# Decode attention and MLP on one core: load targets moved to multiples of 512 bytes, wo read four rows to a partition, the last V in quarters, h1's zeros written early

## The chip, the cores and the metric

The kernel runs on one core of a Trainium2 chip, the other cores idle. The metric is the device time of one execution in microseconds (us), the median of three runs. A profiled execution of the same kernel gives the trace; its span runs from the first instruction to the last.

## The reference

One decoding step of a pre-LayerNorm transformer block: four sequences, one new token each, 32 heads of 128, 4096 cached positions.

```python
x = A_x                                               # (4, 1, 640), all bf16
h = x + attention(_layernorm(x), k_cache, v_cache, wq, wo)
h2 = h + mlp(_layernorm(h), w1, b1, w2)               # the result

def attention(x, k_cache, v_cache, wq, wo):           # caches (4, 32, 4096, 128), wq (640, 4096)
    q = (x @ wq).reshape(B, 1, 32, 128).transpose(0, 2, 1, 3)
    p = softmax(einsum("bhqd,bhkd->bhqk", q, k_cache) * 128 ** -0.5)
    o = einsum("bhqk,bhkd->bhqd", p, v_cache)
    return o.transpose(0, 2, 1, 3).reshape(B, 1, 4096) @ wo    # wo (4096, 640)

def mlp(x, w1, b1, w2):                               # w1 (640, 1728), w2 (1728, 640)
    h = x @ w1 + b1
    return (h * tanh(log1p(exp(-abs(h))) + max(h, 0))) @ w2
```

The two caches are 134 MB each, so nearly all of the work is reading them once.

## The kernel before

**Tiles.** A group `g` (of `NG` = 32) is one sequence and four heads. `load_k(g)` and `load_v(g)` (lines 85 to 100) each bring 4 MB into a tile of 128 partitions by 32 KB: partition `32*q + p` holds 128 successive positions of head `q`. There are two K and two V buffers. For the last group alone, K and V come in `NP` = 2 parts, so that work can start on the first.

**One group.** `mul_and_sum` multiplies K by the broadcast query on VectorE (line 334) and sums over the head's 128 elements by matmuls with the identity (line 341); `finish_sum` and `softmax` make the weights `e2`; `pv_moving` (line 242) multiplies V as the moving operand. For groups 30 and 31 `pv` (line 268) is used: 128 matmuls, one for each position of a partition, V as weights.

**Projection.** `normalise(hq)` writes `otn[:, hq]`, the attention output of four heads with the element `d` on the partitions. `project(hq)` (line 315) adds 20 matmuls to `yT`, with `wo_sb[:, h, :]` as weights, in which partition `p` holds row `128*h + p` of wo. `PROJ_AT` says after which group each `project` runs. wo is loaded in four DMAs after groups 8 to 11 (line 431), eight heads each. A DMA moves one contiguous run at a time; here a run is one row of wo, 1,280 bytes.

**The queue of loads.** All loads but x are issued by SyncE's queue (SP), in program order: wq, then K and V by turns, wo and b1 between them, and at the end (lines 460 to 464) w1, `w2s_sb` (160 KB), `w2r_sb` (the last 64 rows of w2, 80 KB) and w2 in three parts of 640 KB. K of group `g+2` can be issued only when group `g` has been used up, since it overwrites it. The 16 DMA engines each carry 8 partitions of a 128-partition load and work through their own list in order.

**Completion semaphores.** In the built program the loads of SP's queue take eight completion semaphores by turns. A load that takes a semaphore waits, on SP, until the load that had it eight places earlier has landed on all engines. In the tail before, V31's parts have numbers 7 and 0, w1 1, `w2s_sb` 2, `w2r_sb` 3; the parts of w2 have 4, 5 and 6, which the two halves of K31 and V30 had.

**The tail** (lines 467 to 597): softmax of group 31, `pv(30)`, `pv(31)`, `normalise(7)`, `project(7)`, the residual `hT`, its mean (line 488), `h2T` (line 495), 70 matmuls with w1 into `h1_ps` (line 511), the activation, 70 matmuls with w2 into `y2T` (line 573: first `w2s_sb`, then `w2r_sb`, then the three parts of w2), and the store. The last chunk of `h1_ps` has only 64 rows of weights; a memset (line 506) writes zeros in its other 64 rows, and the first matmul of line 511 comes after that memset.

**Where the loads land.** In the built program of before, a partition holds the small constants first, then wq, then the working tiles, then K and V. K starts at byte 93,088 of a partition, which is 160 bytes past a multiple of 256 and 32 past one of 64; the other K and V buffers and `w12` (w1 and w2, in a K buffer) stand the same way. wq and wo start at 48,416 (32 past a multiple of 256, and of 64). `x_bf`, 5 KB, starts at 16,512: a multiple of 128, and not of 256.

Of the kernel before, what the change touches and what calls it, by code (L numbers as in the profile page):

```python
# [8 lines left out]
FP32 = mybir.dt.float32  # L9
BF16 = mybir.dt.bfloat16  # L10
# [6 lines left out]
def kernel(  # L17
# [23 lines left out]
    nc = tc.nc  # L41

    B, Sq, D = A_x.shape
    _, H, Sk, Dh = A_k_cache.shape
    F = B_w1.shape[1]
    N = B * Sq
    DC = D // 128
    G = 4
    PH = 128 // G
    R = Sk // PH  # L50
    NP = 2
    RP = R // NP
    W = 512 // RP
    HQ = H // G
    NG = HQ * N
# [3 lines left out]
    WOC = 8  # L59
# [9 lines left out]
    C2 = F // 128  # L69
    FREM = F - C2 * 128  # L70
    FC = C2 + 1

    ctx.enter_context(tc.manual_schedule())

    consts = ctx.enter_context(tc.tile_pool(name="consts", bufs=1))
    wbig = ctx.enter_context(tc.tile_pool(name="wbig", bufs=1))
    work = ctx.enter_context(tc.tile_pool(name="work", bufs=2))
    kpool = ctx.enter_context(tc.tile_pool(name="kpool", bufs=KBUFS))
    vpool = ctx.enter_context(tc.tile_pool(name="vpool", bufs=VBUFS))

    x_rows = A_x.rearrange("b s d -> (b s) d")
    out_rows = out.rearrange("b s (c p) -> (b s c) p", p=128)


    def load_kv(pool, tag, cache, g):
        hq, b = divmod(g, N)
        t = pool.tile([128, R, Dh], BF16, tag=tag, name=f"{tag}{g}")
        view = cache[b, G * hq : G * (hq + 1)].rearrange("h (p r) d -> (h p) r d", p=PH)

        np_ = NP if g == NG - 1 else 1  # L90
        for i in range(np_):
            r0, r1 = i * R // np_, (i + 1) * R // np_
            nc.sync.dma_start(out=t[:, r0:r1, :], in_=view[:, r0:r1, :])
        return t

    def load_k(g):
        return load_kv(kpool, "kt", A_k_cache, g)

    def load_v(g):
        return load_kv(vpool, "vt", A_v_cache, g)  # L100

    x_bf = consts.tile([N, D], BF16)
    nc.scalar.dma_start(out=x_bf[:, :], in_=x_rows[:, :])
# [9 lines left out]
    ident = consts.tile([128, 128], BF16)  # L113
# [20 lines left out]
    otn = consts.tile([128, HQ, N, G], BF16)  # L134

    for q in range(G):
        nc.vector.tensor_copy(
            out=sel[:, :, q, q * PH : (q + 1) * PH],
            in_=ident[0:N, 0:N].unsqueeze(2).to_broadcast([N, N, PH]),
# [27 lines left out]
    ps = ps_cm.__enter__()  # L167
# [51 lines left out]
    PROJ_AT = {B1_AT + 1 + hq: hq for hq in range(4)}  # L219
# [70 lines left out]
    def normalise(hq):  # L290
        nc.vector.tensor_tensor(
            out=otn[:, hq, :, :],
            in0=ot.pop(hq)[:, :, :],
            in1=rls.pop(hq)[:, :, :],
            op=ALU.mult,
        )
# [3 lines left out]
    def f_chunk(rows, c):  # L300

        if c < CK * CI:
            k, i = divmod(c, CI)
            block = rows[:, k * 128 * CI : (k + 1) * 128 * CI]
            return block.rearrange("p (f i) -> p i f", i=CI)[:, i, :], 128
        return rows[:, c * 128 : min(F, (c + 1) * 128)], min(F - c * 128, 128)

    yT = ps.tile([128, DC, N], FP32, tag="yT")
    wo_sb = []

    def project(hq):

        for h in range(hq * G, (hq + 1) * G):
            for c in range(DC):
                nc.tensor.matmul(
                    yT[:, c, :],
                    lhsT=wo_sb[0][:, h, c * 128 : (c + 1) * 128],
                    rhs=otn[:, hq, :, h % G],
                    start=(h == 0 and c == 0),
                    stop=(h == H - 1 and c == DC - 1),  # L320
                )
# [3 lines left out]
    def mul_and_sum(g, part):  # L325

        hq, b = divmod(g, N)
        r0 = part * RP
        kt = kts[g][:, r0 : r0 + RP, :]
        s_ps = ps.tile([128, RP, W], FP32, tag="s", bufs=2, name=f"s{g}_{part}")  # L330
        s_of[g, part] = s_ps
        for k in range(NQ):
            d0 = k * DQ
            nc.vector.tensor_tensor(  # L334
                out=kt[:, :, d0 : d0 + DQ],
                in0=kt[:, :, d0 : d0 + DQ],
                in1=qbs[:, hq, b, d0 : d0 + DQ].unsqueeze(1).to_broadcast([128, RP, DQ]),
                op=ALU.mult,
            )
            for d in range(d0, d0 + DQ, W):  # L340
                nc.tensor.matmul(  # L341
                    s_ps[:, :, :],
                    lhsT=ident[:, :],
                    rhs=kt[:, :, d : d + W],
                    start=(d == 0),
                    stop=(d == Dh - W),
                )
            yield

    def finish_sum(g, part):  # L350
        if part == 0:
            s_sbs[g] = work.tile([128, R], FP32, tag="s_sb", name=f"s_sb{g}")
        nc.vector.tensor_reduce(  # L353
            out=s_sbs[g][:, part * RP : (part + 1) * RP],
            in_=s_of.pop((g, part))[:, :, :],
            axis=AX.X,
            op=ALU.add,
        )
# [35 lines left out]
    for g in range(NG):  # L394
        hq, b = divmod(g, N)
        for part in range(NP):
            now = mul_and_sum(g, part)
            before = None
            next(now)
            if part > 0:  # L400
                finish_sum(g, part - 1)
                if 2 <= g < NG - NSTAT + 2:
                    add_blocks(g - 2)
                    if b == 1:
                        row_sums(hq - 1)
                        normalise(hq - 1)
            elif g >= 1:
                finish_sum(g - 1, NP - 1)
                before = softmax(g - 1)
                next(before)  # L410
            next(now)
            if before is not None:
                next(before)
        kts.pop(g)
        if g + 2 < NG:
            kts[g + 2] = load_k(g + 2)
        if 1 <= g < NG - NSTAT + 1:
            pv_moving(g - 1)
        if g in PROJ_AT:
            project(PROJ_AT[g])  # L420
        if g + 1 < NG:
            vts[g + 1] = load_v(g + 1)
        for n in Q_AT.get(g, ()):
            q_chunk(n)
            q_broadcast(n)
        if g in WO_AT:

            if not wo_sb:
                wo_sb.append(wbig.tile([128, H, D], BF16, tag="w", name="wo_sb"))
            h0 = WO_AT[g] * WOC  # L430
            nc.sync.dma_start(
                out=wo_sb[0][:, h0 : h0 + WOC, :],
                in_=A_wo.rearrange("(h p) n -> p h n", p=128)[:, h0 : h0 + WOC, :],
            )
            if WO_AT[g] == 0:
                nc.sync.dma_start(out=b1_row[:, :], in_=B_b1.rearrange("(o f) -> o f", o=1))
        if g == B1_AT:
            b_ps = ps.tile([128, FC], FP32, tag="small", name="b_ps")
            for c in range(FC):
                cols, fw = f_chunk(b1_row[:, :], c)  # L440
                nc.tensor.matmul(
                    b_ps[0:fw, c : c + 1],
                    lhsT=cols,
                    rhs=ident[0:1, 0:1],
                    start=True,
                    stop=True,
                )
            nc.vector.tensor_copy(out=b1T[:, 0:C2], in_=b_ps[:, 0:C2])
            nc.vector.tensor_copy(out=b1T[0:FREM, C2:FC], in_=b_ps[0:FREM, C2:FC])
# [7 lines left out]
    w2r_sb = mlp.tile([FREM, D], BF16)  # L457
# [1 line left out]
    w2_view = B_w2[0:FM, :].rearrange("(k p i) n -> p k i n", k=CK, i=CI)  # L459
    nc.sync.dma_start(out=w1_sb, in_=B_w1.rearrange("(c p) n -> p c n", p=128))  # L460
    nc.sync.dma_start(out=w2s_sb[:, :], in_=B_w2[FM : C2 * 128, :])
    nc.sync.dma_start(out=w2r_sb[:, :], in_=B_w2[C2 * 128 : F, :])
    for k in range(CK):
        nc.sync.dma_start(out=w2_sb[:, k], in_=w2_view[:, k])


    finish_sum(NG - 1, NP - 1)
# [26 lines left out]
    for dst in (h2T, hc):  # L494
        nc.vector.tensor_tensor(
            out=dst[:, :, :],
# [5 lines left out]
    nc.vector.tensor_tensor(out=sq[:, :, :], in0=hc[:, :, :], in1=hc[:, :, :], op=ALU.mult)  # L502


    h1_ps = ps.tile([128, FC, N], FP32, tag="qq", name="h1_ps")
    nc.vector.memset(h1_ps[FREM:128, FC - 1, :], 0.0)
    rstd = mlp.tile([128, N], FP32)
    for c in range(FC):
        fw = f_chunk(w1_sb[:, 0, :], c)[1]
        for dc in range(DC):  # L510
            nc.tensor.matmul(  # L511
                h1_ps[0:fw, c, :],
                lhsT=f_chunk(w1_sb[:, dc, :], c)[0],
                rhs=h2T[:, dc, :],
                start=(dc == 0),
                stop=(dc == DC - 1),
            )
        if c == 4:
# [3 lines left out]
                out=std[:, :], in_=v_ps[:, :], func=ACT.Sqrt, bias=eps_t[:, :], scale=1.0  # L522
# [5 lines left out]
        out=h1n[:, :, :],  # L528
# [6 lines left out]
        out=h1s[:, :, :],  # L535
# [9 lines left out]
        out=tb[:, :, :],  # L545
# [8 lines left out]
        out=ta[:, :, :], in0=tb[:, :, :], scalar1=-0.5, scalar2=-1.0, op0=ALU.mult, op1=ALU.add  # L554
# [4 lines left out]
        out=act_t[:, :, :],  # L559
# [10 lines left out]
    for i, (w2, c) in enumerate(w2_of):  # L570
        rows = 128 if c < C2 else FREM
        for dc in range(DC):
            nc.tensor.matmul(  # L573
                y2T[:, dc, :],
                lhsT=w2[:, dc * 128 : (dc + 1) * 128],
                rhs=act_t[0:rows, c, :],
                start=(i == 0 and dc == 0),
                stop=(i == FC - 1 and dc == DC - 1),
# [3 lines left out]
        out=oT[:, :, :].rearrange("p n c -> p c n"),  # L582
# [7 lines left out]
        lhsT=oT[:, :, :].rearrange("p n c -> p (n c)"),  # L590
        rhs=ident[:, :],
        start=True,
        stop=True,
# [35 lines left out]
```

## Time and profile before

| what | us |
|---|---|
| median of three runs (674.6 to 674.92) | 674.84 |
| the profiled execution, whole | 674.36 |
| its span | 672.6 |
| PE busy / DVE busy in the span | 566.7 / 351.6 |

The span is 1.8 us shorter than the execution that it belongs to: start and end lie outside it.

The trace also holds each DMA packet (here one contiguous run) with its time on its engine:

| run | what | packets | shortest, ns | median, ns | mean, ns |
|---|---|---|---|---|---|
| 40,960 B | wq | 128 | 1,514 | 1,514 | 1,605 |
| 32,768 B | K, V | 7,936 | 1,213 | 1,215 | 1,218.5 |
| 16,384 B | halves of K31, V31 | 512 | 611 | 613 | 616 |
| 5,120 B | w2 in three parts | 384 | 196 | 201 | 215 |
| 3,456 B | w1 (and b1) | 641 | 135 | 140 | 145 |
| 1,280 B | wo | 4,096 | 55 | 59 | 59.6 |
| 1,280 B | `x_bf` | 4 | 53 | 53 | 90 |

All 397 K and V packets that began before 44 us took 1,213 ns. In that stretch the next packet of an engine starts 3 to 4 ns before the one ahead of it ends.

And when each load of the tail had landed on its first and on its last engine, by the completion semaphores:

| load | first engine, us | last engine, us |
|---|---|---|
| V30 | 641.2 | 646.4 |
| V31, first half | 646.1 | 651.3 |
| V31, second half | 651.0 | 656.26 |
| w1 | 656.4 | 662.09 |
| `w2s_sb` | 656.9 | 662.69 |
| `w2r_sb` | 657.3 | 663.18 |
| w2, parts 1, 2, 3 | 659.0, 660.6, 662.4 | 664.50, 666.07, 667.63 |

The engines are 5 to 6 us apart there. For w1, six of the 16 landed between 661.4 and 662.09, three at 659.8 to 660.0 and seven between 656.4 and 658.8.

### The profile page before, as it was taken

The page shows a single profiled execution, that of the slowest core. Times are in us where ns is not written, and L with a number is a line of the kernel's source. Part 1 is how long each engine was busy: PE and PEld are TensorE (multiplying, and loading weights), DVE is VectorE, ACT ScalarE, POOL GpSimd, SP SyncE. Part 2 cuts the span into 40 slices and gives each one's busy share as a digit, 9 for nine tenths or more (in the row PEclk, how much of TensorE's full clock was granted, in tenths as well). Part 3 has the DMA queues.
Part 4 walks back from the last instruction along what each step waited for, and adds up shares of the span by engine and source line. Part 5 has one row for each costly group of instructions (what it writes and reads, how often), then busy time and mean ns, then how long its engine had stood idle before and what let it go on. Part 6 is the DMA issues. An engine that isn't in the chain of part 4 may idle for free.

```text
span 672.6 us, 7163 instructions
## 1 busy us (share of the span) xinstructions
PE 566.7 (84%) x3121; PEld 256.1 (38%) x3121; DVE 351.6 (52%) x304; ACT 112.2 (17%) x343; POOL 2.4 (0%) x13
## 2 busy tenths in 40 slices
PE   0589999899998896688999899879988799888985
PEld 0234444344443332233443344333433344333454
DVE  2475445455654356236654545665544566554642
ACT  0022122122210111011110111111111111101231
POOL 1000000000000000000000000000000000000000
PEclk9999999799998987878998899898999799898995
DMA  9999999999999999999999999999999999999995
GB/s 373 437 436 437 430 428 428 426 437 434 432 431 421 422 416 412 441 419 425 430 434 427 433 430 430 431 435 432 431 428 428 433 434 437 428 431 424 433 411 204
DMA packets 15191, 283.81 MB, mean 422 GB/s; under 512 B 1267, under 2 KB 5559, under 8 KB 6584
## 3 DMA queue, kind: packets, MB, share of 16 engines
q1 hardware_dynamic: 15152, 283.36, 98.8%
q8 instruction: 24, 0.39, 0.2%
q14 instruction: 7, 0.06, 0.0%
q10 hardware_dynamic: 8, 0.01, 0.0%
HBM read 283.35 MB, written 0.01 MB: 421 GB/s over the span
## 4 chain that ended last, share of the span: by engine, by line
DMA 43%; PE 37%; DVE 18%; issue 1%; ACT 1%; SPq 0%; DVEq 0%
DMA kt<-in_A_k_cache_dram 41%; PE s L341 19%; DVE kt L334 15%; PE p L242 11%; PE ot L256 3%; DMA vt<-in_A_v_cache_dram 3%; PE q_ps L188 1%; PE qb_ps L202 1%; DVE s_sb L353 1%; PE tr L366 1%; DVE mx L371 1%; ACT q_all L195 1%; PE h_ps L511 0%; PE l_ps L280 0%; PE y2T L573 0%
## 5 line engine op out<-in xcount | busy, mean ns | idle before, releaser
L334 DVE TENSOR_TENSOR kt<-kt,qbs 128x4096 bf16<-128x4096 bf16 x128 | 291.4, 2278 | 222.8 <-DMA kt<-in_A_k_cache_dram 222.8
L341 PE MATMUL s<-kt,ident 128*128 128x512 bf16 x1024 | 267.4, 408 | 75.8 <-DVE kt L334 75.6
L242 PE MATMUL p<-vt,e 128*16 128x512 bf16 x960 | 214.2, 382 | 0.0
L341 PEld LDWEIGHTS <-ident 128*128 128x128 bf16 x1024 | 99.7, 103 | 199.5 <-issue 100.6
L242 PEld LDWEIGHTS <-e 128*16 128x16 bf16 x960 | 84.3, 90 | 129.8 <-issue 17.8
L384 ACT ACTIVATE e<-s_sb,nbs 32x128 bf16<-32x128 f32 x128 | 73.9, 577 | 2.5
L250 ACT COPY p_sb<-p 16x512 f32<-16x512 f32 x30 | 17.2, 574 | 316.6 <-PE p L242 316.6
L353 DVE TENSOR_REDUCE s_sb<-s 128x64 f32<-128x512 f32 x64 | 43.4, 678 | 3.4 <-PE s L341 3.3
L381 ACT COPY nbs<-tr 128x4 f32<-128x4 f32 x32 | 5.2, 162 | 177.4 <-PE tr L379 177.4
L256 PEld LDWEIGHTS ot<-ident_f,p_sb 16*128 16x128 f32 x240 | 28.9, 186 | 12.7 <-issue 12.7
L384 ACT ACTIVATION_READ_ACCUMULATOR e<-s_sb,nbs 32x1 f32 x128 | 32.1, 251 | 0.0
L256 PE MATMUL ot<-ident_f,p_sb 16*128 16x4 f32 x240 | 31.5, 250 | 0.0
L371 DVE TENSOR_REDUCE mx<-tr 1x4 f32<-1x128 f32 x32 | 8.9, 277 | 41.4 <-PE tr L366 41.3
L188 PE MATMUL q_ps<-wq_sb,xT 128*4 128x512 bf16 x40 | 11.0, 409 | 9.7 <-DMA wq_sb<-in_A_wq_dram 9.7
L366 PE MATMUL tr<-ident_f,pm 128*1 128x128 f32 x64 | 13.7, 300 | 1.2 <-DVE pm L364 1.2
L379 PEld LDWEIGHTS tr<-mx,nscale 1*128 1x128 f32 x64 | 9.4, 182 | 13.8 <-issue 12.7
L288 DVE RECIPROCAL rl<-l_ps 128x16 f32<-128x16 f32 x8 | 2.1, 257 | 23.1 <-PE l_ps L280 23.1
L202 PE MATMUL qb_ps<-q_all,sel 4*128 4x128 bf16 x128 | 9.2, 225 | 5.3 <-ACT q_all L195 5.3
L379 PE MATMUL tr<-mx,nscale 1*128 1x4 f32 x64 | 12.2, 258 | 0.4 <-DVE mx L371 0.4
L202 PEld LDWEIGHTS <-sel 4*128 4x128 bf16 x128 | 8.4, 98 | 9.1 <-issue 9.1
L195 ACT CAST q_all<-q_ps 4x512 bf16<-4x512 f32 x8 | 4.6, 574 | 34.6 <-PE q_ps L188 34.6
L366 PEld LDWEIGHTS tr<-ident_f,pm 128*1 128x1 f32 x64 | 2.8, 81 | 18.4 <-issue 18.4
(79 smaller groups left out, 81.5 us busy)
## 6 DMA issues: line engine op xcount, KB each, us to landing
kt<-in_A_k_cache_dram SPq DMA_DIRECT2D x31, 4096.0 KB, 24.5
vt<-in_A_v_cache_dram SPq DMA_DIRECT2D x31, 4096.0 KB, 27.7
wq_sb<-in_A_wq_dram SPq DMA_DIRECT2D x1, 5120.0 KB, 15.3
wo_sb<-in_A_wo_dram SPq DMA_DIRECT2D x4, 1280.0 KB, 30.5
kt<-in_A_k_cache_dram SPq DMA_DIRECT2D x2, 2048.0 KB, 19.6
vt<-in_A_v_cache_dram SPq DMA_DIRECT2D x2, 2048.0 KB
w<-in_B_w_dram SPq DMA_DIRECT2D x1, 2160.0 KB, 22.9
w<-in_B_w_dram SPq DMA_DIRECT2D x3, 640.0 KB, 19.8
```

The costliest lines, as they stand in the source:

```text
L188: nc.tensor.matmul(q_ps[:, :], lhsT=xT[:, c, :], rhs=wq_sb[:, c, n * QC : (n + 1) * QC], start=(c == 0), stop=(c == DC - 1),)
L202: nc.tensor.matmul(qb_ps[:, b * Dh : (b + 1) * Dh], lhsT=sel[:, b, q, :], rhs=q_all[:, h * Dh : (h + 1) * Dh], start=(q == 0), stop=(q == ...
L242: nc.tensor.matmul(p_ps[:, :], lhsT=e2[g % NE2][:, r : r + J, :].rearrange("p j q -> p (j q)"), rhs=vt[:, r : r + J, :].rearrange("p j d - ...
L250: nc.scalar.copy(out=blocks[g][:, :], in_=p_ps[:, :])
L256: nc.tensor.matmul(o, lhsT=p_sb[:, j * Dh : (j + 1) * Dh], rhs=ident_f[0 : J * G, j * G : (j + 1) * G], start=(j == 0), stop=(j == J - 1),)
L334: nc.vector.tensor_tensor(out=kt[:, :, d0 : d0 + DQ], in0=kt[:, :, d0 : d0 + DQ], in1=qbs[:, hq, b, d0 : d0 + DQ].unsqueeze(1).to_broadcas ...
L341: nc.tensor.matmul(s_ps[:, :, :], lhsT=ident[:, :], rhs=kt[:, :, d : d + W], start=(d == 0), stop=(d == Dh - W),)
L353: nc.vector.tensor_reduce(out=s_sbs[g][:, part * RP : (part + 1) * RP], in_=s_of.pop((g, part))[:, :, :], axis=AX.X, op=ALU.add,)
L366: nc.tensor.matmul(tr_ps[0:1, 0:128], lhsT=pm[:, :], rhs=ident_f[:, :], start=True, stop=True)
L371: nc.vector.tensor_reduce(out=mx[:, :], in_=tr_ps[0:1, 0:128].rearrange("o (a b) -> o a b", a=G), axis=AX.X, op=ALU.max,)
L379: nc.tensor.matmul(nb_ps, lhsT=nscale[:, :], rhs=mx[:, :], start=True, stop=True)
L384: nc.scalar.activation(out=e2[g % NE2][p0:p1, :, q], in_=s_sb[p0:p1, :], func=ACT.Exp, bias=nb[p0:p1, q : q + 1], scale=SCALE, accum_out=r ...
```

## The change

Four edits in the words of the title, and one more in the diff.

- **Order of the pools.** A 384-byte pad, then K and V, then wq/wo, then the constants. In the built program K and V now start at 16,896, 49,664, 82,432 and 115,200, and wq and wo at 147,968: all multiples of 512. `w2s_sb` starts at a multiple of 512, `w2r_sb` at one of 256.
- **wo.** Eight DMAs of four heads in place of four of eight. In the first seven, partition `p` holds rows `4*p` to `4*p + 3` of a block of 512 rows, one run of 5,120 bytes; the last keeps the old order. `regroup(hq)`, new, rearranges `otn[:, hq]` to match: 16 matmuls with strided columns of the identity, each into 32 partitions, and one VectorE copy into `o4`. It runs in the same group as the `project` that reads it, before it.
- **The last V** in four parts; the last K stays in two.
- **The memset** of `h1_ps` stands before the last softmax.
- **`w2r_sb`** is loaded in eleven DMAs of 10, 9, 9, 8, 7, 6, 5, 4, 3, 2 and 1 rows, ahead of the three parts of w2 in SP's queue.

With the additional DMAs the eight semaphores fall otherwise in the tail. As built, the parts of V31 have 3, 4, 5 and 6, w1 has 7, `w2s_sb` 0. The eleven pieces (called r0 to r10 here) have 1 to 7, 0, 1, 2, 3, and the parts of w2 have 4, 5 and 6 again. So the waits are: r0 for K31's second half, r1 for V30, r2 to r5 for the four parts of V31, r6 for w1, r7 for `w2s_sb`, r8 to r10 for r0 to r2, and the three parts of w2 for r3, r4 and r5.

PE has 112 more matmuls and as many weight loads.

```diff
-    consts = ctx.enter_context(tc.tile_pool(name="consts", bufs=1))
-    wbig = ctx.enter_context(tc.tile_pool(name="wbig", bufs=1))
-    work = ctx.enter_context(tc.tile_pool(name="work", bufs=2))
+    pad = ctx.enter_context(tc.tile_pool(name="pad", bufs=1))
+    pad.tile([128, 192], BF16, name="pad")
     kpool = ctx.enter_context(tc.tile_pool(name="kpool", bufs=KBUFS))
     vpool = ctx.enter_context(tc.tile_pool(name="vpool", bufs=VBUFS))
+    wbig = ctx.enter_context(tc.tile_pool(name="wbig", bufs=1))
+    consts = ctx.enter_context(tc.tile_pool(name="consts", bufs=1))
+    work = ctx.enter_context(tc.tile_pool(name="work", bufs=2))
...
-    def load_kv(pool, tag, cache, g):
+    def load_kv(pool, tag, cache, g, parts):
...
-        np_ = NP if g == NG - 1 else 1
+        np_ = parts if g == NG - 1 else 1
...
-        return load_kv(kpool, "kt", A_k_cache, g)
+        return load_kv(kpool, "kt", A_k_cache, g, NP)
...
-        return load_kv(vpool, "vt", A_v_cache, g)
+        return load_kv(vpool, "vt", A_v_cache, g, 2 * NP)
...
+    o4 = consts.tile([128, HQ - 1, G, N], BF16)
+    ident4 = ident[:, :].rearrange("p (j i) -> p i j", i=G)
+
+    def regroup(hq):
+        o4_ps = ps.tile([128, G, N], FP32, tag="small", name=f"o4_{hq}")
+        for q in range(G):
+            for i in range(G):
+                nc.tensor.matmul(
+                    o4_ps[q * PH : (q + 1) * PH, i, :],
+                    lhsT=ident4[:, i, :],
+                    rhs=otn[:, hq, :, q],
+                    start=True,
+                    stop=True,
+                )
+        nc.vector.tensor_copy(out=o4[:, hq, :, :], in_=o4_ps[:, :, :])
...
-                    rhs=otn[:, hq, :, h % G],
+                    rhs=o4[:, hq, h % G, :] if hq < HQ - 1 else otn[:, hq, :, h % G],
...
+                if g in PROJ_AT:
+                    regroup(PROJ_AT[g])
...
-            nc.sync.dma_start(
-                out=wo_sb[0][:, h0 : h0 + WOC, :],
-                in_=A_wo.rearrange("(h p) n -> p h n", p=128)[:, h0 : h0 + WOC, :],
-            )
+            for h in range(h0, h0 + WOC, G):
+                order = "(p i) n -> p i n" if h + G < H else "(i p) n -> p i n"
+                nc.sync.dma_start(
+                    out=wo_sb[0][:, h : h + G, :],
+                    in_=A_wo[h * Dh : (h + G) * Dh, :].rearrange(order, i=G),
+                )
...
-    nc.sync.dma_start(out=w2r_sb[:, :], in_=B_w2[C2 * 128 : F, :])
+    p0 = 0
+    for n in (10, 9, 9, 8, 7, 6, 5, 4, 3, 2, 1):
+        nc.sync.dma_start(
+            out=w2r_sb[p0 : p0 + n, :], in_=B_w2[C2 * 128 + p0 : C2 * 128 + p0 + n, :]
+        )
+        p0 += n
     for k in range(CK):
         nc.sync.dma_start(out=w2_sb[:, k], in_=w2_view[:, k])
+
+    h1_ps = ps.tile([128, FC, N], FP32, tag="qq", name="h1_ps")
+    nc.vector.memset(h1_ps[FREM:128, FC - 1, :], 0.0)
...
-    h1_ps = ps.tile([128, FC, N], FP32, tag="qq", name="h1_ps")
-    nc.vector.memset(h1_ps[FREM:128, FC - 1, :], 0.0)
```

## The prediction

> **What bounds the kernel now.** I read the page's row of DMA shares first, then its queues, and then the tail: the chain of waits, the landings and the timeline.
>
> ```profile
> DMA  9999999999999999999999999999999999999995
> GB/s 373 437 436 437 430 428 428 426 437 434 432 431 421 422 416 412 441 419 425 430 434 427 433 430 430 431 435 432 431 428 428 433 434 437 428 431 424 433 411 204
> q1 hardware_dynamic: 15152, 283.36, 98.8%
> ```
>
> The DMA engines are full in 39 of 40 slices. Engine time taken off any load ahead of the tail brings the tail forward by as much; time taken off another engine brings nothing while loads are queued. PE is busy 566.7 of 672.6 us, so it has room.
>
> The end of the chain of waits (start, length, what):
>
> ```profile
> 638.66 17.60 DMA vt<-in_A_v_cache_dram
> 656.52 1.05 issue
> 657.57 1.81 PE ot L268 x62
> 659.63 0.69 PE yT L315 x20
> 660.79 0.60 PE mean_ps L488 x2
> 662.13 0.97 PE h_ps L511 x25
> ...
> 667.37 2.20 PE y2T L573 x70
> ```
>
> It names V31's second half, 656.26, as the last wait. The timeline shows another wait just as late:
>
> ```profile
> 661.42 0.17 DVE L495 TENSOR_TENSOR h2T<-hT,mean_ps 128x20 bf16<-128x20 f32 x1 [0.68 <-PE mean_ps L488]
> 661.90 0.06 DVE L506 MEMSET h_ps<- 64x4 f32 x1
> 662.13 0.89 PEld L511 LDWEIGHTS <-w 128*128 128x128 bf16 x25 [0.84 <-DMA w<-in_B_w_dram]
> 662.13 0.97 PE L511 MATMUL h_ps<-h2T,w 128*128 128x4 bf16 x25 [0.75 <-DVE var_part L484]
> ```
>
> h2T is ready at 661.59, the zeros at 661.96, but w1's weights landed on the last engine at 662.09, and line 511 started 0.04 later. So w1's landing on the slowest engine, which I call T1, sets h1. From there the tail is computation, down to y2T's end at 669.56 (last weights landed at 667.63, 1.3 us before their matmuls).
>
> **The parts of the change.**
>
> *wo in long runs.* Before, an engine carries 256 runs of 1,280 B. At 59.6 ns less the 4 ns by which one overlaps the next: 256 x 55.6 = 14.2 us. After: 7 x 8 = 56 runs of 5,120 B at 201 - 4 = 197 ns (w2's rows) and 32 of the old kind: 11.0 + 1.8 = 12.8. That is 1.4 us saved; with w2's mean of 215 it is 0.6, with its shortest of 196 it is 1.7. I take 1.3. The doubled number of wo issues waits for semaphores now: the fourth one waits for K10. At that moment V9, two wo loads, K11, V10 and a wo load, some 14 MB or over 30 us at 430 GB/s, are queued behind K10, and the K load that SP holds back behind that wait needs K10 landed and used anyway. So this costs nothing; if the cover were gone, a late K would show as idle DMA.
>
> *regroup.* 7 x 16 matmuls and 7 copies. The nearest row, line 268, does 128 such matmuls in 3.43 us, so 0.43 us each time, and the copy about 0.2 us like line 291 (0.18). Hidden by the same surplus of queued loads: K takes a median of 24.5 us from issue to landing, of which its own 4 MB are 9.7, so some 15 us of loads stand ahead of it. If nothing hid it, 7 x 0.7 = 5 us. PE's 228 more instructions are one 16 KB fetch more. It takes an engine 0.6 us (613 ns for such a run), and six of 16 engines are the late ones: 0.2 us expected, 0 to 0.6.
>
> *Aligned targets.* The trace of before has no load aligned so, and this is the largest unknown. Shortest times of 1,280 and 40,960 B, 55 and 1,514 ns, give 0.03677 ns a byte and 8 ns for a run whatever its size; 32,768 B at 1,213, 16,384 at 611, 5,120 at 196 and 3,456 at 135 lie on that line within 1 ns. So a target off alignment costs nothing in proportion to its bytes that a size would show, and what can vanish is at most the 8 ns of a run. The one row with a better start is `x_bf`, at a multiple of 128: 53 ns where the others need 55. Up to T1 an engine carries 528 runs of K and V (quarters counted), 8 of wq, 88 of wo and 40 of w1: 664. The ends are 664 x 0 = 0 and 664 x 8 = 5.3 us. `x_bf`, the nearest, says 2 ns, 1.3 us, but it is not at a multiple of 512 and others are; I take 4 ns, half of the fixed part: 2.7 us. No reason for a loss: the buffers and what reads them stay the same.
>
> [...]
>
> *V31 in quarters, and the memset.* With three quarters done when the last lands, 32 matmuls remain instead of 64, and the 1.05 us of "issue" would fall before the last landing: h2T could come about 2 us earlier. It is worth 0.04 us, because w1 lands at 662.09 either way. 16 more runs for an engine cost 16 x 4 ns = 0.1 us. The memset's 0.06 us on VectorE falls where that engine waits 1.99 us.
>
> *w2r in eleven pieces.* This is the part that costs. Before, SP had issued everything by 649 us:
>
> ```profile
> 638.28 0.80 SPq L93 DMA_DIRECT2D vt<-in_A_v_cache_dram  x2
> 639.18 0.39 SPq L460 DMA_DIRECT2D w<-in_B_w_dram  x1
> 639.61 1.17 SPq L461 DMA_DIRECT2D w2s_sb<-in_B_w_dram  x1
> 640.83 3.78 SPq L462 DMA_DIRECT2D w2r_sb<-in_B_w_dram  x1
> 644.65 4.70 SPq L464 DMA_DIRECT2D w<-in_B_w_dram  x3
> ```
>
> After, r0 to r5 wait for V31's parts or earlier, which lies under w1's transfer. But r6 waits for w1 itself, T1, and r7 for `w2s_sb`, 0.6 later by the landings. Behind it in SP's queue stand r8, r9, r10 and the three parts of w2, whose other waits are met by then. One issue follows another after 0.42 us (638.28, 638.70; 639.18, 639.61). So w2's first part is issued at T1 + 0.6 + 4 x 0.42 = T1 + 2.3. From issue to the first packet on an idle engine: wq was issued at 0.73 and its first packets began at 1.75 on the first engine and 2.40 on the last, 1.0 to 1.7. The three parts need 1.57 us each by their landings, 4.7 together. They land at T1 + 8.0 to 8.7, say T1 + 8.35 = 670.44 where T1 is unmoved. Then the last 20 matmuls at 29 ns remain, 0.6: y2T ends at 671.05 instead of 669.56. That is +1.5; +0.9 if issues take 0.33 and the engines start together, +2.6 if an instruction fetch (the last one took 1.4 us) comes between. The engines stand idle meanwhile; store and end follow as before.
>
> [...] The rows above show issues 0.42 us apart, without waiting for each other's landing.
>
> *Sum.* T1 moves by -1.3 - 2.7 + 0.1 + 0.2 = -3.7; the tail adds 1.5: -2.2 us. Against the profiled execution, 674.36, that is 672.2; the median stands 0.48 above it, so 672.6.
>
> **Rivals.**
> 1. *Alignment gives only what `x_bf` shows.* 2 ns, 1.3 us: -2.3 + 1.5 = -0.8, 674.0, which cannot be told from no change. For it: the only row that shows anything. Against: no load of before was at 512.
> 2. *Slower: w2 becomes the last wait and nothing pays for it.* Runs keep their 1,213 ns, and the late issue of w2 costs its upper end: -1.3 + 0.1 + 0.2 + 2.6 = +1.6, 676.4. For it: the line through all sizes leaves little to gain, and the issue order is certain. It decides if a run is shortened by less than 0.4 ns and the first packet of w2 comes over 4 us after T1.
> 3. *More than the fixed part goes.* Since 44 us a K or V run takes 1,218.5 on average, not 1,213; if alignment ends that too, 528 x 5.5 = 2.9 us more and the fixed 8 ns: -1.3 - 5.3 - 2.9 + 0.3 + 1.5 = -7.7, 667.1. Against it: the 397 runs before 44 us were just as unaligned and undisturbed, so the disturbance has another cause.
> 4. *The quarters and the memset pay their 2 us.* Only if w1 were early; its landing at 662.09 says no.
>
> **How the numbers follow.** The measurement tells 0.2%, 1.35 us, from no change: 673.5 and 676.2 are the borders. Forecast (4 ns a run, its neighbourhood 671 to 673.5): 0.52. Rival 1: 0.2. Rival 2: 0.22. Rival 3: 0.05. Rival 4: 0.01. Faster is the forecast with rivals 3 and 4, 0.58; same 0.20; slower 0.22. The range goes from the forecast with all of the fixed part gone (-1.3 - 5.3 + 0.3 + 1.5 = -4.8, 670.0) to rival 2's 676.4.
>
> **What would show it.** Shortest K and V runs at 1,209 ns or so (1,211 is rival 1, 1,213 rival 2). Mean of wo's slices above their 412 to 416 GB/s. Line 96's last V landing 3 to 4 us earlier than 656.26. SP's eleven issues with a gap ending at w1's landing, and y2T's matmuls waiting for a DMA where before they waited for VectorE only. If h1's matmuls start with h2T rather than with w1, or w2 is issued before w1 has landed, the tail's sum is wrong.

## The result, and the profile after

The changed kernel takes 678.77 us (median of six runs, 677.82 to 680.51) where the kernel before takes 674.88 (six runs, 674.57 to 676.19): a ratio of 1.0058, with a 95% interval of 1.0041 to 1.0075. It is slower, and lies 2.4 us above the end of the predicted range. The profiled execution, 680.05 us with a span of 678.3, is one of the slower runs.

The page's DMA rows after:

```profile
DMA  8999999999999999999999999999999999999993
GB/s 371 433 434 433 434 432 432 434 434 433 434 432 420 450 420 443 410 445 432 433 421 376 401 398 428 433 432 433 432 430 437 432 432 433 430 431 421 429 376 146
DMA packets 12904, 283.83 MB, mean 418 GB/s; under 512 B 1411, under 2 KB 2119, under 8 KB 4040
q1 hardware_dynamic: 12864, 283.36, 97.6%
```

In slices 2 to 12 the rates are steadier than before, 432 to 434 GB/s. But slices 22 to 24 (some 356 to 407 us) have 376, 401 and 398, and slice 39 has 376: here the engines ran out of queued loads (their busy share is 0.90, 0.93 and 0.96 in the first three, 0.95 in the last, and 1.00 in slice 25), which no slice before the tail showed in the old kernel. The page's chain, by engine, says what held the loads back (before: DMA 43%, PE 37%):

```profile
PE 61%; DMA 19%; DVE 18%; issue 1%; ACT 1%; SPq 0%; DVEq 0%
```

So the bound has moved from the loads to PE: from 279 to 576 us the chain after holds no load, where the one before has seven waits for K that begin there. The rows of q1 say the same: 98.8% of 672.6 us before and 97.6% of 678.3 after are 664.5 and 662.0 us, so the loads took 2.5 us less of the engines' time, and the engines stood idle 8.2 us more. VectorE's waits, in the view of who waited for whom (total us, times, longest), show a new one. Before:

```profile
DVE kt L334 <- DMA kt<-in_A_k_cache_dram: 222.8, 30, 19.2
DVE mx L371 <- PE tr L366: 41.3, 23, 6.1
DVE rl L288 <- PE l_ps L280: 23.1, 8, 4.3
```

After:

```profile
DVE kt L354 <- DMA kt<-in_A_k_cache_dram: 136.5, 25, 18.9
DVE mx L391 <- PE tr L386: 108.6, 29, 7.5
DVE rl L291 <- PE l_ps L283: 23.1, 8, 4.3
DVE o L326 <- PE o L319: 16.5, 7, 2.7
```

Line 326 is the copy into `o4`. VectorE stood 16.5 us in front of seven of these copies, 2.4 us each, and waited 86 us less for K to land: K is there, and PE is late. The timeline after shows one of the seven, in group 30 (start, length, engine, line; in brackets the idle time before it):

```profile
628.03 1.89 PE L361 MATMUL s<-kt,ident 128*128 128x512 bf16 x8 [0.43 <-DVE kt L354]
...
629.85 1.05 PE L259 MATMUL ot<-ident_f,p_sb 16*128 16x4 f32 x8
...
630.83 0.33 PE L319 MATMUL o<-otn,ident 128*32 128x4 bf16 x16
...
631.25 0.17 DVE L326 CAST o<-o 128x16 bf16<-128x16 f32 x1 [2.67 <-PE o L319]
631.35 4.48 DVE L354 TENSOR_TENSOR kt<-kt,qbs 128x4096 bf16<-128x4096 bf16 x2
633.68 2.79 PE L361 MATMUL s<-kt,ident 128*128 128x512 bf16 x8 [2.52 <-DVE kt L354]
```

And the same place before, where VectorE went straight on to the second half of the product:

```profile
626.55 1.89 PE L341 MATMUL s<-kt,ident 128*128 128x512 bf16 x8 [0.42 <-DVE kt L334]
...
627.02 2.27 DVE L334 TENSOR_TENSOR kt<-kt,qbs 128x4096 bf16<-128x4096 bf16 x1
...
628.36 1.05 PE L256 MATMUL ot<-ident_f,p_sb 16*128 16x4 f32 x8
...
629.35 1.90 PE L341 MATMUL s<-kt,ident 128*128 128x512 bf16 x8
```

After the change the copy stands on VectorE ahead of that product, and it needs regroup's matmuls, which stand on PE behind eight score matmuls and `add_blocks`. So VectorE waits 2.67 us, then makes the product late, and PE, with nothing else to do, waits 2.52 us. Its eight score matmuls then take 2.79 us instead of 1.90. The clock records of the trace tell why: from 634.5 to 637.9 us PE was granted half its clock. Such half-clock windows, 3.4 or 6.8 us long, add up to 81.9 us ahead of the tail, against 68.3 before; seven of them (at 320.5, 341.0, 364.9, 385.3, 480.9, 556.0 and 634.5) follow the seven regroups.

### The profile page after: what moved, and what is told of

It is laid out like the page before. It is cut to its first block, busy times and chain, and to the rows that moved or that the text cites. A ratio compares the mean times of both kernels' runs of the same rounds, so it can differ in the third digit from the quotient of the medians.

```text
span 678.3 us, 7413 instructions
## 1 busy us (share of the span) xinstructions
PE 575.2 (85%) x3233; PEld 259.5 (38%) x3233; DVE 353.4 (52%) x311; ACT 112.1 (17%) x343; POOL 2.4 (0%) x13
## 3 DMA queue, kind: packets, MB, share of 16 engines
q1 hardware_dynamic: 12864, 283.36, 97.6%
## 4 chain that ended last, share of the span: by engine, by line
PE 61%; DMA 19%; DVE 18%; issue 1%; ACT 1%; SPq 0%; DVEq 0%
PE s L361 26%; PE p L245 26%; DVE kt L354 16%; DMA kt<-in_A_k_cache_dram 15%; PE ot L259 4%; DMA w2s_sb<-in_B_w_dram 3%; PE tr L386 1%; PE q_ps L191 1%; DVE mx L391 1%; PE qb_ps L205 1%; DMA w<-in_B_w_dram 1%; PE yT L335 1%; ACT q_all L198 1%; DVE s_sb L373 0%; PE o L319 0%
## 5 line engine op out<-in xcount | busy, mean ns | idle before, releaser
L245 PE MATMUL p<-vt,e 128*16 128x512 bf16 x960 | 220.1, 389 | 0.0
L361 PEld LDWEIGHTS <-ident 128*128 128x128 bf16 x1024 | 99.8, 103 | 196.6 <-issue 102.9
L245 PEld LDWEIGHTS <-e 128*16 128x16 bf16 x960 | 85.7, 92 | 137.1 <-issue 29.3
L399 PEld LDWEIGHTS tr<-mx,nscale 1*128 1x128 f32 x64 | 9.4, 183 | 13.8 <-issue 13.1
L291 DVE RECIPROCAL rl<-l_ps 128x16 f32<-128x16 f32 x8 | 2.1, 257 | 23.1 <-PE l_ps L283 23.1
L326 DVE CAST o<-o 128x16 bf16<-128x16 f32 x7 | 1.2, 174 | 16.5 <-PE o L319 16.5
```

Source lines behind the costliest of these rows:

```text
L245: nc.tensor.matmul(p_ps[:, :], lhsT=e2[g % NE2][:, r : r + J, :].rearrange("p j q -> p (j q)"), rhs=vt[:, r : r + J, :].rearrange("p j d - ...
L361: nc.tensor.matmul(s_ps[:, :, :], lhsT=ident[:, :], rhs=kt[:, :, d : d + W], start=(d == 0), stop=(d == Dh - W),)
L399: nc.tensor.matmul(nb_ps, lhsT=nscale[:, :], rhs=mx[:, :], start=True, stop=True)
```

## The experiments

Theory S: the order of the copy on VectorE makes PE run dry, and its clock halves; the loads themselves became faster. Theory W: the loss is w2's late issue behind the eleven pieces of w2r, which the prediction had as its way to a slower kernel. Theory C: PE's clock fell for another reason. All ratios are to the kernel before, on the same chip, with their 95% intervals. In the first four:

**Copies on ScalarE.**

```diff
-        nc.vector.tensor_copy(out=o4[:, hq, :, :], in_=o4_ps[:, :, :])
+        nc.scalar.copy(out=o4[:, hq, :, :], in_=o4_ps[:, :, :])
```

> The changed kernel, with the seven copies of regroup into o4 made by ScalarE instead of VectorE; all matmuls stay. Theory S (stall): in the changed kernel VectorE waits some 2.4 us in front of each of these copies, because the copy needs matmuls that stand behind the score matmuls in PE's order; the second half of the K product is late by that, PE runs dry for about 2.5 us, and its clock falls to half for 3.4 or 6.8 us. Then this edit alone brings back nearly all of the loss and shows the gain of the loads: 672 to 674.5 us, VectorE's 16.5 us of waiting for regroup gone, K issued early enough that no slice of the DMA row falls below 410 GB/s. Theory W (the eleven pieces of w2r hold back w2): no change, 678 to 679.5. Theory C (the granted clock fell for another reason, such as PE's extra matmuls themselves): no change or 1 us at most.

672.81 us, ratio 0.996 (0.9946 to 0.9973). One changed engine name takes 6.0 us off the changed kernel by the medians, 6.6 by the ratios. The half-clock windows ahead of the tail fall to 47.8 us, and none follows a regroup. The chain again has seven waits for K that begin between 279 and 576 us. Of what was expected, only the DMA row missed: its slice 39, in which the tail begins, has 406 GB/s. The same place in its timeline, with the copy off VectorE's path:

```profile
624.44 1.05 PE L259 MATMUL ot<-ident_f,p_sb 16*128 16x4 f32 x8
...
625.42 0.33 PE L319 MATMUL o<-otn,ident 128*32 128x4 bf16 x16
...
625.68 1.90 PE L361 MATMUL s<-kt,ident 128*128 128x512 bf16 x8
625.85 0.17 ACT L326 CAST o<-o 128x16 bf16<-128x16 f32 x1 [1.06 <-PE o L319]
```

The score matmuls follow regroup without a gap, at full speed. The matmuls of regroup cost PE 0.33 us. Theories W and C fail here.

**w2r in one DMA.**

```diff
-    p0 = 0
-    for n in (10, 9, 9, 8, 7, 6, 5, 4, 3, 2, 1):
...
+    nc.sync.dma_start(out=w2r_sb[:, :], in_=B_w2[C2 * 128 : F, :])
```

> The changed kernel, with w2r loaded by one DMA as before. Theory S: PE is late by 5 us when the tail begins, so w2 is needed late as well and its late issue costs only the 0.2 us that y2T's matmuls wait for it: 678 to 679, at most 0.5 us below the changed kernel. Theory W: the loss was here, 674 to 676.

678.59 us, ratio 1.0047 (1.0034 to 1.0059), against 678.77 and 1.0058 for the changed kernel, with intervals that overlap: the pieces are not what made it slower.

**Pools alone.** The kernel before with the new order of pools.

> The kernel before, with the pools in the new order and nothing else: every large load lands at a multiple of 512. In the changed kernel the shortest K or V run took 1,211 ns instead of 1,213 and the mean where nothing starved was 1,214 instead of 1,218.5, so 528 x 4 ns = 2 us. Theory S: 672.5 to 673.3, with the runs' mean at 1,214. Theory C (faster loads by themselves bring down PE's clock): 675 or more, with a clock below the 0.935 of before.

671.92 us, ratio 0.9949 (0.9936 to 0.9961): 3.4 us faster, more than the 2.7 us of the prediction and the 2 us expected here. Packets, from the traces:

| run | before, mean ns | pools alone, mean ns | shortest, both | runs of an engine | saved, us |
|---|---|---|---|---|---|
| 32,768 B | 1,218.5 | 1,214.6 | 1,213 | 512 | 2.0 |
| 1,280 B (wo) | 59.6 | 55.2 | 55 and 53 | 256 | 1.1 |
| 3,456 B (w1) | 145 | 138.3 | 135 | 40 | 0.3 |

Together 3.4 us, the whole gain. (The 512 count both halves of a split tile as one.) The shortest runs stay as they were, but for 2 ns at wo; what goes is the difference between shortest and mean. Of the K and V runs 37% took over 1,216 ns before, and 0.5% now. Theory C, which had faster loads bring down the clock, fails again: the granted clock of its runs, 0.934 to 0.945, is no lower than that of the kernel before, 0.932 to 0.945.

**Regroup alone.** The kernel before, with regroup in the places it has in the changed kernel.

```diff
+                if g in PROJ_AT:
+                    regroup(PROJ_AT[g])
```

> The kernel before, with regroup run in the same places as in the changed kernel, its result unused: wo keeps its old order, and addresses, queue and tail stay. Theory S: slower than before by the whole loss, 677.5 to 681, with VectorE waiting some 16 us for regroup and more half-clock windows in the trace. Theory W: 675 to 675.5, the loads hide it.

681.69 us, ratio 1.0091 (1.0075 to 1.0107), 6 us slower and 0.7 above the range expected, with the same 16.5 us in front of the copies:

```profile
DVE o L323 <- PE o L316: 16.5, 7, 2.7
```

So regroup as placed loses 6 us, with the addresses and the loads left alone. How much of it is the pause itself and how much the clock no run separates: here the half-clock windows ahead of the tail add up to 71.7 us, 3.4 more than before, and one of the seven pauses (319.4 to 322.0) has none. Then four more, two of them repairs.

**Both repairs**: copies on ScalarE and w2r in one DMA.

> The changed kernel with both repairs: regroup's copies on ScalarE and w2r in one DMA. With the copies on ScalarE alone (672.8 us) the matmuls of y2T took 4.8 us from first to last instead of 2.2, waiting for w2's parts. Theory S with the pieces as a second, smaller loss: 2.4 us below that kernel, 670.4 (669.6 to 671.2), and faster than the aligned pools alone (671.9). If the pieces cost nothing: 672.5 or more.

670.74 us, ratio 0.9931 (0.9917 to 0.9945): 4.7 us faster than before, the fastest of all by the median; its interval overlaps that of the pools alone. The pieces cost 2.1 us where PE is not late. y2T's matmuls in the kernel with the pieces (copies on ScalarE):

```profile
663.26 0.28 PE L604 MATMUL y2T<-act_t,w2s_sb 128*128 128x4 bf16 x5 [2.10 <-DVE act_t L589]
...
663.90 0.69 PE L604 MATMUL y2T<-act_t,w 128*128 128x4 bf16 x20
...
665.81 0.69 PE L604 MATMUL y2T<-act_t,w 128*128 128x4 bf16 x20 [1.22 <-DMA w<-in_B_w_dram]
...
667.35 0.70 PE L604 MATMUL y2T<-act_t,w 128*128 128x4 bf16 x20 [0.85 <-DMA w<-in_B_w_dram]
```

and in the one with both repairs, without a wait:

```profile
664.40 0.29 PE L599 MATMUL y2T<-act_t,w2r_sb 64*128 64x4 bf16 x5
...
664.62 1.76 PE L599 MATMUL y2T<-act_t,w 128*128 128x4 bf16 x60
```

**The same without quarters and early zeros.**

```diff
-        return load_kv(vpool, "vt", A_v_cache, g, 2 * NP)
+        return load_kv(vpool, "vt", A_v_cache, g, NP)
...
-    h1_ps = ps.tile([128, FC, N], FP32, tag="qq", name="h1_ps")
-    nc.vector.memset(h1_ps[FREM:128, FC - 1, :], 0.0)
...
+    h1_ps = ps.tile([128, FC, N], FP32, tag="qq", name="h1_ps")
+    nc.vector.memset(h1_ps[FREM:128, FC - 1, :], 0.0)
     rstd = mlp.tile([128, N], FP32)
```

> As the kernel with both repairs, but the last V in two parts and h1's zeros written where they were before: what remains of the change is the alignment and wo in long runs. If the quarters and the zeros are worth next to nothing, as predicted: 670.4 to 671.1, the zeros alone 0.25 us by the wait that the aligned kernel still shows at its first h1 matmul. If the quarters pay their 2 us: 672 or more.

671.26 us, ratio 0.9933 (0.9921 to 0.9946). The two edits together cannot be told from nothing. The quarters don't pay even here, where w1 no longer lands last, because PE does not wait for V: in this kernel, with V31 in halves, it goes through the first 82 matmuls of `pv(31)`, 18 of them with the second half, without a wait. Then it stands still, with quarters too, though V31's last packet had ended at 651.5 and 651.4 us. In the kernel with both repairs and in this one:

```profile
654.93 1.36 PE L271 MATMUL ot<-e,vt 128*128 128x4 bf16 x46 [1.41 <-issue]
```

```profile
651.34 2.33 PE L271 MATMUL ot<-e,vt 128*128 128x4 bf16 x82
...
654.89 1.37 PE L271 MATMUL ot<-e,vt 128*128 128x4 bf16 x46 [1.23 <-issue]
```

**The pieces alone.** The kernel before with w2r in eleven pieces.

> The kernel before, with w2r loaded in the eleven pieces and nothing else. w2's parts are issued only after w1 has landed. By the prediction's tail sum 1.5 us slower than before (0.9 to 2.6), by the wait measured in the changed kernel with ScalarE's copies 2.6: 676.2 to 677.8. If the loss of the pieces is only there when PE is early, no change: 675.2.

677.38 us, ratio 1.0022 (1.0013 to 1.0032): 1.5 us slower by the ratio, by the medians 1.7. In its trace y2T's matmuls wait for w2 three times, 0.16, 0.50 and 0.87 us. But w2's parts take 7.1 us from their first packet (664.39) to the end of their last (671.48), and the activation that y2T also needs comes 1.2 us later than before.

**Regroup after the product.**

```diff
-                if g in PROJ_AT:
-                    regroup(PROJ_AT[g])
...
             next(now)
+            if part > 0 and g in PROJ_AT:
+                regroup(PROJ_AT[g])
```

> The changed kernel with regroup issued after the second half of the K product instead of ahead of it, VectorE still making the copies and w2r still in pieces. Theory S says that the order hurts, not the engine or the added work: VectorE's copy now stands behind the product that PE waits for, so 672.4 to 674, like the kernel with ScalarE's copies (672.8). If it is VectorE's added work or PE's added matmuls: 677 to 679.

673.08 us, ratio 0.9961 (0.9947 to 0.9975), as with ScalarE's copies. VectorE does the copies again, and the same matmuls run; only their order against the product has changed. It is the order that cost 6 us. VectorE waits in front of its copies no less than before:

```profile
DVE o L326 <- PE o L319: 17.4, 7, 3.5
```

The wait alone costs nothing that shows. It costs where the product that PE needs next stands behind it.

The last three ask what of the alignment counts, with the pools in the new order and another pad.

```diff
-    pad.tile([128, 192], BF16, name="pad")
+    pad.tile([128, 112], BF16, name="pad")
```

> The kernel before with the pools in the new order, but a pad of 224 bytes instead of 384: all large targets stand 32 bytes past a multiple of 64 again, as before. With the pad of 384 it took 671.9 us. If the alignment is the cause: back to 674.5 to 675.7, with K and V runs at 1,218 ns on average and wo's rows at 59 to 60. If the order of the pools or the moved constants are the cause: 671.5 to 672.5.

676.08 us, ratio 1.0009 (1.0 to 1.0018); K and V runs take 1,218.5 ns on average, wo's rows 59.1. The order of the pools brings nothing.

With 224 elements in place of 192:

> The same with a pad of 448 bytes: K, V, wq, wo, w1 and w2 start 64 bytes past a multiple of 512, so at multiples of 64 and no more. If 64 is what counts: 671.5 to 672.7, K and V runs at 1,214 to 1,215 ns on average. If it has to be 256 or 512: 674.5 to 675.7 and 1,218 ns; a share of the gain if the number of parts into which a run falls counts.

674.63 us, ratio 0.9997 (0.9989 to 1.0006); 1,218.6 and 59.3 ns. 64 is not enough.

With 320:

> The same with a pad of 640 bytes: the large targets start 256 bytes past a multiple of 512. If 256 is enough: 671.5 to 672.7 and 1,214 to 1,215 ns. If it has to be 512: 674 or more.

671.85 us, ratio 0.9949 (0.9938 to 0.9961); 1,214.6 and 55.2 ns. A multiple of 256 gave all that one of 512 gave. Not every load stands so: w1's five runs in a partition follow each other after 3,456 bytes, 13.5 times 256, so the second and the fourth start 128 bytes past a multiple of 256 when the first starts at one, and w2's parts do too. Of the 641 runs of that size 551 took the shortest time, 135 ns, with the pools alone (72 in the kernel before, 194 with the pad of 448 bytes), so at least 166 of the 256 that stood at 128 did. Multiples of 128 may be enough, then; no run moved the other loads to them.

## Why the prediction was wrong

The effects found, put in a row: with both repairs the change takes 670.7 us, 4.7 less than before by its ratio; the pieces add 2.1 (672.8), and the order of regroup's copies 6.0 more (678.8), by the medians; by the ratios these two are 2.0 and 6.6.

- **What bounds the kernel.** Right for the kernel before, but not something that would stay. PE worked 566.7 of 672.6 us, and the prediction took the rest for room. It is room only while PE is not made to wait: in the changed kernel the chain of waits holds no load from 279 to 576 us, and PE and the product set the pace there.
- **regroup, the step that failed.** The prediction priced its operations rightly (0.43 us a time for the matmuls, 0.33 measured; 0.2 for the copy, 0.17 measured), called them hidden by some 15 us of queued loads, and entered them in the sum with nothing but an instruction fetch. It did not ask what stands behind the copy on VectorE and whom the copy itself waits for. With its wait the copy holds VectorE for 2.5 us, not 0.2, and the product behind it is late by that; PE stands idle 2.5 us each time, and its clock falls on top. The whole costs 6 us, with regroup alone as in the changed kernel. That the prediction's 5 us for operations that nothing hides lies near is luck: the same operations run on PE and VectorE in the kernel with regroup behind the product, and cost nothing there that the runs could show. The fetch is in the trace, 25 packets of 16 KB for 24, of 0.93 us on average in place of the 0.6 taken from a load's run; its share of the time was not measured. Four regroups in consecutive groups, 14 to 17, and their stalls used up the queued loads, as slices 22 to 24 show, and the one in group 30 falls just ahead of slice 39 with its 376 GB/s. A row of before showed the price: `row_sums` and its reciprocal on VectorE are built the same way, and line 288 waited 23.1 us for PE in eight times, with a half-clock window after that of group 29 at 611.8.
- **Aligned targets.** The size was near, 2.7 us forecast and 3.4 measured, but by luck, for the reasoning was wrong: the 8 ns that the line of shortest times leaves for every run did not shrink (the shortest of K and V stayed at 1,213 with the pools alone). What went was some 4 of the 5.5 ns by which the mean lies above the shortest time (1,218.5 to 1,214.6, over 1,213), a scatter which the third rival named and the prediction set aside because unaligned runs before 44 us showed none. Those runs show only that the scatter needs something more than a bad address, not that the address has no part in it. The row of `x_bf`, 53 against 55 ns, said nothing about it: with targets out of line too, the kernel before with the pieces has 53 as its shortest. Nor does the sign of the first rival, a shortest K or V run of 1,211 ns: the changed kernel has it, and so has the kernel before with regroup, with its targets out of line. How far past a multiple of 256 K and V stood, 160 bytes in the kernel before or 64 in the run with a pad of 448 bytes, did not show: 1,218.5 and 1,218.6 ns on average. (The 528 runs of K and V are those with V31 in halves; in quarters it is 544, which at 4 ns each is under 0.1 us.)
- **wo in long runs.** 1.3 us forecast. Once aligned, its short rows cost 55.2 ns, not 59.6, so less is left: 256 x 51.2 = 13.1 us against 56 x 192.6 + 32 x 51 = 12.4, 0.7 us, from wo's packets in the kernel without quarters (196.6 ns for a long run, less the overlap of 4). That kernel is 0.7 us below the aligned pools by the medians, with intervals that overlap.
- **w2r in pieces.** Forecast 1.5 us (0.9 to 2.6); 1.5 to 1.7 in the kernel before, 2.1 in the changed one without its stall. That the size fits is in part luck: with the pieces alone w2's parts took 7.1 us, not 4.7, and the activation was late as well. The order of the issues was foreseen: in the changed kernel SP stood 4.9 us until w1 had landed, and issued the rest 0.3 to 0.4 us apart. In that kernel the loss is hidden: PE is so late that w2 is there in time but for 0.2 us.
- **V in quarters, and the zeros.** Forecast to bring next to nothing, and they do. The reason given, w1 landing last, holds for the kernel before; once the loads or PE have moved, h1 starts with h2T, which the prediction named as a sign that its tail's sum is wrong. The 2 us that it saw behind that were not there: before, PE waited 0.33 us for V31's second half, and the 1.05 us of "issue" is no wait for V.
- **The rivals.** The second had the sign, and named w2's late issue. The runs refute it as the cause: w2r in one DMA leaves the changed kernel at 678.6 us.

## What to carry to other kernels

When a small operation is added to an engine that works in order, as VectorE did here with the copies of 0.17 us that waited 2.4 us each, look past its length: at what it waits for, what stands behind it, and who waits for that. A producer that another engine feeds on belongs ahead of an operation which waits for that same engine, or the operation belongs on an idle engine: by the medians the first took 5.7 us off the changed kernel, the second 6.0. Where loads are the bound, try their targets at multiples of 256 bytes in a partition (3.4 us here by the ratio, and nothing at multiples of 64), and judge packets by their mean, not only by the shortest: K and V runs went from 1,218.5 to 1,214.6 ns on average, and the shortest stayed at 1,213.

## What the runs showed of the hardware

- With the large targets at multiples of 256 bytes (pad of 640 bytes) 32 KB runs took 1,214.6 ns on average instead of 1,218.5, wo's runs of 1,280 bytes 55.2 instead of 59.6, and the kernel 3.4 us less by its ratio. Targets at multiples of 64 and no more (pad of 448) saved nothing: 1,218.6 and 59.3 ns, a ratio of 0.9997. Nothing of it shows before 44 us, when 397 K and V runs of the kernel before and 397 of the changed one took 1,213 ns, every one; why the scatter begins then was not tried.
- PE's granted clock fell to half at each of the seven pauses of 2.5 us in the changed kernel, for 3.4 us or twice that, which makes a stall cost more than its own length: the score matmuls took 2.79 us instead of 1.90. The length of a pause does not decide it alone: one of 3.69 us (515.7 to 519.4, pools alone) had no half clock behind it. In all thirteen traces the changes of the clock lie on a grid of 3.41 us. Between 60 and 640 us, with pauses over 1 us counted, 126 of the 127 steps of that grid at full clock in which PE was idle for over 60% were followed by half clock, and none of the 1,670 with under 10%; between these, some were and some not.
- PE's gap in `pv(31)`, 1.05 us before and 1.23 to 1.95 in others, is put down to no wait by the trace. In all thirteen traces a 16 KB packet of the queue for instructions ends within 0.5 us of its start, and PE goes on 1.30 to 1.49 us after that end (before: packet from 655.04 to 656.15, pause from 656.52 to 657.57). So PE probably waits for its instructions there; no run moved the fetch, and it is not shown.
